# Attention, a gated MLP and an eight-expert layer on one core: a unit's keys and queries issued earlier, a spread of embeddings issued elsewhere

## The chip, the cores and the metric

The kernel runs on one core of a Trainium2 chip: TensorE (PE) for matrix products, VectorE (DVE), ScalarE (ACT), GpSimd (POOL), and SyncE (SP), which here issues nearly all transfers. The metric is the device time of one execution in microseconds; the comparison is between medians of runs.

## The reference

Three layers follow each other, all in float32.

```
scores = (q @ k^T) / sqrt(64) + bias(head, distance)   # only 0 <= distance < 128
x   = softmax(scores) @ v                              # 4 x 8 heads x 576 x 64 -> 2304 x 512
h   = x @ w_in                                         # 512 -> 2048
y   = (h * clip(h + 3, 0, 6) / 6) @ w_out              # 2048 -> 512
logits = (y/|y|) @ (emb/|emb|)^T / tau                 # 8 experts
e   = argmax(logits);  gate = softmax(logits)[e]
out = gate * (relu(y @ w1[e]) @ w2[e])                 # 512 -> 1024 -> 512, each token by its expert
```

## The kernel before

The 2304 tokens are cut into nine chunks of 256. Attention is done in units: a unit is one chunk and one pair of heads, so a chunk has four units, and unit n belongs to chunk n // 4. Units 0 to 7 (chunks 0 and 1, class `Early`) come from staged blocks. Units from 8 on (class `Unit`) load their own keys `kr`, queries `qr` and values `vr` in small pieces (`load_k`, `load_q`, `load_v`; L562 for keys and queries, L582 and L584 for values). Each of these tiles has two buffers, so a unit's load waits until the unit two before it has given its tile back.

A unit's path is: DVE transposes the keys to `kT` (L590) and the queries to `qT` (L594), ACT scales `qT` (L601), PE makes the scores `sc_ps` (L610), DVE and ACT make the softmax (L620 to L643), PE transposes it ("flips", L649), ACT and POOL bring it into order, and PE multiplies it with the values (`acc`, L675). PE does the flips of one unit, the values of the unit before it and the scores of the unit after it as one group.

The first MLP product is gemm1 (`h_ps`, L720; plain in chunk 0, L707), the second gemm2 (`y_ps`, L773; plain L764). A block of gemm1 goes through a relu on ACT (L730), a gate on DVE (L740) and a split into a high and a low part, `gh` on ACT (L744) and `gl` on DVE (L750), before gemm2 can take it. Weights are split the same way (L349 on ACT, L355 on DVE).

Behind a chunk's last gemm2 ACT copies its rows to `ys` (L792), SP stores them (L797), and the chunk is routed. For chunks 0 to 6 the logits are dot products on DVE (L834) of the rows with the normalised embeddings, which a spread (`spread`, L828) brings to all 128 partitions: a transfer of 1 MB for each half of the experts, so two per chunk. A spread's target `en_all` comes from the pool `w` of 17 large buffers, in which weight pieces live too. Then come `choose`, `ranks` (L880) and `place`.

The order of the work is made in two ways. For the opening (chunks 0 and 1, units 8 to 12, and unit 13 as far as its scores) the function `plan` holds a list of tasks with engine, duration, rank, needs and buffers taken and given; a small simulation runs them, the ready task of lowest rank first, and the order that it finds is what ACT, DVE and SP are given. Loads of units in it run up to `AHEAD_UNITS`, in the order of the ranks `UNIT_LOADS`; the two spreads of chunk 0 are the tasks `("issue spread", x)`. All later steps are put into `todo` at a place by number (`at(step, ...)`) and follow behind the whole list; PE keeps the written order throughout, and each engine works its own list strictly in order. There the spreads of chunk c stand at `g + loads[x]`, where `g = ends(c)` is the chunk's end, `DOTS` gives `loads = (-3.5, 4.5)`, and the chunk's rows are stored at `g`.

Of the kernel before, what the change touches and what calls it, by code (L numbers as in the profile page):

```python
# [16 lines left out]
SP = mybir.EngineType.SP  # L17
# [22 lines left out]
SPLIT_RANK = (322.3, 398.0, 346.4, 387.6, 346.1, 414.2, 437.7, 461.4, 636.9, 424.0, 421.1, 490.0, 548.3, 371.5, 669.2, 694.1)  # L40
CONST_RANK = (40.0, 50.0)

AHEAD_UNITS = 14

EARLY_CHUNKS = 2
WEIGH = (1, 1, 1, 0, 1, 1, 0, 1)
# [6 lines left out]
UNIT_8 = (95.0, 150.0, 96.0)  # L53
EMBED = (96.0, 97.0)
SOFT_1, DOTS_0 = 250.0, 2000.0
UNIT_LOADS = (80.0, 81.0, 82.0, 83.0, 84.0, 85.0)
FIRST = (16.97, 1.91, 3.35)


# [38 lines left out]
def tile_kernel(  # L98
# [17 lines left out]
    NE = w1.shape[0]  # L116
# [78 lines left out]
    for kinds in ((2, 2), (2, 0), (2, 1), (1, 2), (0, 2)):  # L195
        tables[kinds] = t = const.tile([128, 192], BF16, name="table%d%d" % kinds)
        for h, kind in enumerate(kinds):
            r = slice(64 * h, 64 * h + 64)
# [959 lines left out]
    def at(step, fn, *args):  # L1158
        todo[step].append((fn, args))
# [8 lines left out]
    def ends(c, i=NF2 - 1):  # L1168
        return 0.0 if c == 0 else begins(2) if c == 1 else begins(c, i) + FIRST[2]
# [8 lines left out]
    route_0 = Route(0)  # L1178

    def plan():  # L1180
# [19 lines left out]
        for n in range(len(pieces)):  # L1200
            r = PIECE_RANK[n]
# [5 lines left out]
        for n, u in enumerate(units[:n_early]):  # L1207
            c, p = u.c, u.p
            r = UNIT_RANK[n]
# [18 lines left out]
        for i in range(NF2):  # L1228
            r, d = GEMM_RANK[0][i], GEMM_RANK[1][i]
# [5 lines left out]
        for n in range(len(pieces)):  # L1235
            kind, i = pieces[n]
            r = SPLIT_RANK[n]
# [5 lines left out]
        task(("constants",), "SP", 1.6, CONST_RANK[0], [("issue", "st", 8)], ["w"], ["w"], constants)  # L1243
        for n in range(n_early, AHEAD_UNITS):
            u = units[n]
# [4 lines left out]
        def step(name, engine, cost, rank, needs, takes, gives, fn, *args, lag=0.12):  # L1250
            task(name, engine, cost, rank, needs, takes, gives, fn, args, lag)
# [4 lines left out]
        for n in range(n_early, last_unit + 2):  # L1256
            u, key = units[n], ("unit", n)
            first = n == n_early
            r = UNIT_8[0] if first else SOFT_1 + n
# [5 lines left out]
            r = UNIT_8[2] if first else SOFT_1 - 10  # L1265
# [26 lines left out]
        for x in ORDER_1:  # L1292
            before = line[-1:]
            if x == "u":
# [3 lines left out]
                r = SOFT_1 - 20 + i  # L1298
# [33 lines left out]
            step(("row store", t), "SP", 0.55, 0.0, [("row", t)], [], [], route_0.store, t)  # L1332
        step(("norms",), "ACT", 1.5, 1900.0, [("row", 1)], ["f"], [], route_0.norms)
        for x in range(2):
            step(("issue spread", x), "SP", 0.55, 90.0, [("en", "store"), ("issue", "st", 15)] + ([("dots", NE // 2 - 1)] if x else []), ["w"], [], route_0.spread, x)
            step(("spread", x), "DMA", 4.8, 0.0, [("issue spread", x)], [], [], None, lag=1.0)
        for e in range(NE):
            x, y = divmod(e, NE // 2)
# [43 lines left out]
    for n, u in enumerate(units[n_early:], n_early):  # L1382

        t0, t1, t2 = (group(n + x) for x in range(3))
        turn, norm, early, vearly = PARTS
        if n >= AHEAD_UNITS:
            at(t0 - early, u.load)
# [23 lines left out]
    for c in range(NCH - 1):  # L1411
        g = ends(c)
        if c < NCH - 2:
            loads, *halves, d2, d3 = DOTS
            if c == 0:
                g, r = FIRST[0], route_0
            else:
                r = Route(c)
                at(g, r.rows)
                at(g + 0.3, r.norms)  # L1420
                for x in range(2):
                    at(g + loads[x], r.spread, x)
                for e in range(NE):
                    x, y = divmod(e, NE // 2)
                    at(g + halves[x][0] + halves[x][1] * y, r.dots, e)
            at(g + d2 * (c > 0), r.choose)
            at(g + d3 * (c > 0) + PLACE_C * (c == 0), r.ranks)
            at(g + d3 * (c > 0) + PLACE_C * (c == 0), r.place)
            continue
        r = Route(c)  # L1430
        at(g, r.rows)
        d = ROUTE
        assert 0 < d[0] <= d[1] <= d[2] < d[2] + TOTAL < d[3]
        at(g + d[0], r.flip, 0)
        at(g + d[1], r.flip, 1)
        at(g + d[1], r.norms)
        at(g + d[2], r.logits)
        at(g + d[2] + TOTAL, r.total)
        at(g + d[2] + TOTAL, r.choose)
        at(g + d[3], r.ranks)  # L1440
        at(g + d[3], r.place)
    g = begins(NCH - 1)
# [19 lines left out]
    g = ends(NCH - 1)  # L1462
# [8 lines left out]
    r = Route(NCH - 1)  # L1471
# [34 lines left out]
    for j in range(1, NE):  # L1506
# [6 lines left out]
        if j == 1:  # L1513
            s = PLACE_1
            loads = [s[0] + s[1] * i for i in range(4)]
            splits = [s[2] + s[3] * i for i in range(8)]
            ids, gets, turns = LATE[0] + 0.05, [s[4] + s[5] * t for t in range(n)], [s[8] + s[9] * t for t in range(n)]
        else:
            s = [x + b - 16 for x in NEXT]
            s[5], s[7], s[9] = NEXT[5], NEXT[7], NEXT[9]  # L1520
            loads = [s[0], s[1], s[2], s[3]]
# [155 lines left out]
```

## Time and profile before

| | |
|---|---|
| Median of 3 runs | 780.51 us (778.58 to 782.57) |
| The profiled execution | 778.85 us |
| its span | 777.1 us |
| PE busy | 748.5 us (96%) |
| DVE busy | 522.6 us (67%) |
| ACT busy | 383.8 us (49%) |
| POOL busy | 195.7 us (25%) |
| mean granted clock of TensorE | 0.989 |

The span goes from the first to the last instruction of the profiled execution, whose own time is 1.75 us longer. PE is the engine with the most work; its matmuls are pipelined, so a busy PE is not PE at its peak. What matters for a change of order is where an engine stands idle and what ended the idle time. Granted clock 1.00 is 2.4 GHz, 0.50 is 1.2 GHz.

### The profile page before, as it was taken

The page shows a single profiled execution, that of the slowest core. Times are in us where ns is not written, and L with a number is a line of the kernel's source. Part 1 is how long each engine was busy: PE and PEld are TensorE (multiplying, and loading weights), DVE is VectorE, ACT ScalarE, POOL GpSimd, SP SyncE. Part 2 cuts the span into 40 slices and gives each one's busy share as a digit, 9 for nine tenths or more (in the row PEclk, how much of TensorE's full clock was granted, in tenths as well). Part 3 has the DMA queues.
Part 4 walks back from the last instruction along what each step waited for, and adds up shares of the span by engine and source line. Part 5 has one row for each costly group of instructions (what it writes and reads, how often), then busy time and mean ns, then how long its engine had stood idle before and what let it go on. Part 6 is the DMA issues. An engine that isn't in the chain of part 4 may idle for free.

```text
span 777.1 us, 15993 instructions
## 1 busy us (share of the span) xinstructions
PE 748.5 (96%) x5740; PEld 659.8 (85%) x5740; DVE 522.6 (67%) x1528; ACT 383.8 (49%) x896; POOL 195.7 (25%) x349
## 2 busy tenths in 40 slices
PE   8999999959999999999999999999989999999995
PEld 6566678848888888888888889888889999999994
DVE  4999999885778668688687783356636636645620
ACT  6958665543454544645544542447435544543510
POOL 3000023431241242241422422030323122223211
PEclk9999999979999999999999999999999999999999
DMA  9987242353544443345353220078177446546200
GB/s 211 346 287 210 56 111 43 100 117 87 113 92 132 108 126 72 92 122 136 66 140 98 85 65 2 29 215 276 36 265 255 150 155 198 197 160 215 89 27 28
DMA packets 159110, 103.20 MB, mean 133 GB/s; under 512 B 119419, under 2 KB 135931, under 8 KB 157232
## 3 DMA queue, kind: packets, MB, share of 16 engines
q1 hardware_dynamic: 155280, 92.53, 42.2%
q0 software_dynamic: 3744, 9.58, 3.7%
q8 instruction: 47, 0.77, 0.4%
q14 instruction: 39, 0.32, 0.1%
HBM read 87.71 MB, written 14.47 MB: 131 GB/s over the span
## 4 chain that ended last, share of the span: by engine, by line
PE 67%; DMA 11%; DVE 8%; issue 7%; SPq 3%; ACT 2%; POOL 1%; POOLq 0%; DVEq 0%; ACTq 0%
PE y_ps L773 21%; PE h_ps L720 21%; PE ps_u L1043 7%; PE ps_o L1067 4%; PE ps_z L1125 3%; PE acc L675 3%; DMA out_dram<-ob,ids 2%; PE sc_ps L610 2%; DMA ids<-slots 2%; DMA xg<-ybuf,ids 2%; DMA wst<-in_moe_w_out_dram 2%; DMA slots<-pays,dest 2%; PE ps_pt L649 1%; SPq L562 1%; DVE w L335 1%
## 5 line engine op out<-in xcount | busy, mean ns | idle before, releaser
L720 PEld LDWEIGHTS h_ps<-xs,w_i 128*128 128x128 f32 x1536 | 192.4, 191 | 6.1 <-issue 1.2
L720 PE MATMUL h_ps<-xs,w_i 128*128 128x256 f32 x1536 | 195.2, 283 | 0.0
L773 PE MATMUL y_ps<-w_o,gh 128*128 128x512 f32 x512 | 164.1, 402 | 0.3 <-ACT gh L744 0.3
L664 POOL TENSOR_SCALAR_AFFINE_SELECT ph<-ph 64x128 f32<-64x128 f32 x224 | 95.5, 426 | 193.9 <-ACT ph L656 156.6
L773 PEld LDWEIGHTS y_ps<-w_o,gh 128*128 128x128 f32 x512 | 92.4, 190 | 24.4 <-issue 6.0
L1043 PE MATMUL ps_u<-x,w_e 128*128 128x280 f32 (+5 forms) x768 | 105.4, 294 | 0.0
L162 DVE TENSOR_TENSOR w_e<-st,w_e 128x1024 fp32r<-128x1024 f32 x64 | 76.5, 1217 | 38.6 <-ACT w_e L161 38.6
L773 PE MATMUL y_ps<-w_o,gl 128*128 128x512 f32 x256 | 100.6, 393 | 1.2 <-DVE gl L750 1.2
L1043 PEld LDWEIGHTS ps_u<-x,w_e 128*128 128x128 f32 x768 | 100.5, 189 | 0.2
L834 DVE CUSTOM_DVE_ANT_0 junk<-ys,en_all 128x512 f32<-128x512 f32 x112 | 77.2, 690 | 19.2 <-DMA en_all<-en_rows 10.5
L730 ACT ACTIVATE u<-h_ps,three 128x512 f32<-128x512 f32 x72 | 49.1, 682 | 75.1 <-PE h_ps L720 50.9
L1067 PE MATMUL ps_o<-hs,w_e 128*128 128x280 f32 (+4 forms) x576 | 78.5, 295 | 0.0
L1067 PEld LDWEIGHTS ps_o<-hs,w_e 128*128 128x128 f32 x576 | 76.6, 188 | 0.0
L161 ACT CAST w_e<-st 128x1024 fp32r<-128x1024 f32 x64 | 65.4, 1048 | 17.8 <-DMA st<-in_moe_w_dram 6.3
L740 DVE SCALAR_TENSOR_TENSOR u<-u,h_ps 128x512 f32<-128x512 f32 x72 | 49.2, 684 | 36.3 <-ACT u L730 35.6
L744 ACT CAST gh<-u 128x512 fp32r<-128x512 f32 x64 | 39.7, 620 | 54.1 <-DVE u L740 53.7
L750 DVE TENSOR_TENSOR gl<-u,gh 128x512 fp32r<-128x512 f32 x64 | 45.0, 703 | 26.0 <-ACT gh L744 26.0
L633 ACT ACTIVATE pt<-pt,nm 128x128 f32<-128x128 f32 x112 | 44.1, 395 | 34.3 <-DVE pt L626 33.7
L773 PEld LDWEIGHTS y_ps<-w_o,gl 128*128 128x128 f32 x256 | 48.4, 189 | 13.3 <-DVE gl L750 2.5
L1142 POOL DMA_INDIRECT out_dram<-ob,ids x23 | 30.3, 1317 | 113.5 <-DVE ob L1141 101.9
L1051 ACT ACTIVATE hs<-ps_u 128x280 fp32r<-128x280 f32 (+5 forms) x64 | 25.6, 403 | 45.0 <-PE ps_u L1043 44.0
L1052 DVE SCALAR_TENSOR_TENSOR hs<-ps_u,hs 128x280 fp32r<-128x280 f32 (+5 forms) x64 | 27.8, 443 | 20.6 <-ACT hs L1051 20.2
(185 smaller groups left out, 994.7 us busy)
## 6 DMA issues: line engine op xcount, KB each, us to landing
st<-in_moe_w_dram SPq DMA_DIRECT2D x32, 512.0 KB
st<-in_moe_w_dram SPq DMA_DIRECT2D x16, 1024.0 KB
en_all<-en_rows SPq DMA_DIRECT2D x14, 1024.0 KB
wst<-in_moe_w_in_dram SPq DMA_DIRECT2D x8, 1024.0 KB
wst<-in_moe_w_out_dram SPq DMA_DIRECT2D x8, 1024.0 KB
ybuf<-ys SPq DMA_DIRECT2D x18, 256.0 KB
out_dram<-empty SPq DMA_DIRECT2D x18, 256.0 KB
kr<-in_k_dram SPq DMA_DIRECT2D x48, 48.0 KB
```

Of the source, the lines that this page charges most:

```text
L161: nc.scalar.copy(hi, src)
L162: eng.tensor_tensor(out=lo, in0=src, in1=words(hi), op=ALU.subtract)
L633: nc.scalar.activation(out=x, in_=x, func=AF.Exp, scale=-1.0, bias=nm[:, j:j + 1], accum_out=sums[h][:, j:j + 1])
L664: nc.gpsimd.affine_select(out=out, in_=x, compare_op=ALU.is_gt if out is prev else ALU.is_ge, fill=0.0, base=0, pattern=[[0, 2], [-1 if ou ...
L720: nc.tensor.matmul(hp[:, f, :], lhsT=w[:, a, kk, f * 128:(f + 1) * 128], rhs=xs[:, b, kk, :], start=(n == 0), stop=(n == 3 * KD - 1),)
L730: nc.scalar.activation(out=u, in_=hp, func=AF.Relu, bias=three, scale=1.0)
L740: V.scalar_tensor_tensor(out=u, in0=u, scalar=6.0, in1=h_t[c, i], op0=ALU.min, op1=ALU.mult)
L750: V.tensor_tensor(out=gl, in0=g, in1=words(gh), op=ALU.subtract)
L773: nc.tensor.matmul(y_t[c][t], lhsT=g[a][:, f, t * 128:(t + 1) * 128], rhs=w[:, b, f, :], start=(i == 0 and f == 0 and n == 0), stop=(i == ...
L834: V.tensor_tensor_reduce(out=self.junk, in0=self.ys[t], in1=self.en[:, e % (NE // 2), :], scale=1.0, scalar=0.0, op0=ALU.mult, op1=ALU.add ...
L1043: nc.tensor.matmul(ps, lhsT=w[:, a, kk, (f % 2) * 128:(f % 2) * 128 + 128], rhs=x[:, b, kk, c0:c1], start=(n == 0), stop=(n == 3 * KD - 1),)
L1067: nc.tensor.matmul(ps, lhsT=ws_t[j, 4 + f // 2][:, a, f % 2, d * 128:(d + 1) * 128], rhs=hs[:, b, f, 0:width(j)], start=(n == 0), stop=(n ...
```

## The change

Three numbers and one expression change. `AHEAD_UNITS` goes from 14 to 15, with one more rank in `UNIT_LOADS`: the keys and queries of unit 14 become tasks of the opening's list, where before they were a step of `todo`. Its transpositions stay in `todo`. The two spreads of chunk 0 get rank 70 instead of 90, which puts the first of them before the loads of unit 9 (rank 81). And the first spread of chunk 1 stands at `g + 0.6` instead of `g - 3.5`, that is behind the storing of that chunk's rows at `g` and not before it; the spreads of later chunks stay.

```diff
--- before.py
+++ after.py
@@ -40,7 +40,7 @@
 SPLIT_RANK = (322.3, 398.0, 346.4, 387.6, 346.1, 414.2, 437.7, 461.4, 636.9, 424.0, 421.1, 490.0, 548.3, 371.5, 669.2, 694.1)
 CONST_RANK = (40.0, 50.0)
 
-AHEAD_UNITS = 14
+AHEAD_UNITS = 15
 
 EARLY_CHUNKS = 2
 WEIGH = (1, 1, 1, 0, 1, 1, 0, 1)
@@ -53,7 +53,7 @@
 UNIT_8 = (95.0, 150.0, 96.0)
 EMBED = (96.0, 97.0)
 SOFT_1, DOTS_0 = 250.0, 2000.0
-UNIT_LOADS = (80.0, 81.0, 82.0, 83.0, 84.0, 85.0)
+UNIT_LOADS = (80.0, 81.0, 82.0, 83.0, 84.0, 85.0, 86.0)
 FIRST = (16.97, 1.91, 3.35)
 
 
@@ -1332,7 +1332,7 @@
             step(("row store", t), "SP", 0.55, 0.0, [("row", t)], [], [], route_0.store, t)
         step(("norms",), "ACT", 1.5, 1900.0, [("row", 1)], ["f"], [], route_0.norms)
         for x in range(2):
-            step(("issue spread", x), "SP", 0.55, 90.0, [("en", "store"), ("issue", "st", 15)] + ([("dots", NE // 2 - 1)] if x else []), ["w"], [], route_0.spread, x)
+            step(("issue spread", x), "SP", 0.55, 70.0, [("en", "store"), ("issue", "st", 15)] + ([("dots", NE // 2 - 1)] if x else []), ["w"], [], route_0.spread, x)
             step(("spread", x), "DMA", 4.8, 0.0, [("issue spread", x)], [], [], None, lag=1.0)
         for e in range(NE):
             x, y = divmod(e, NE // 2)
@@ -1419,7 +1419,7 @@
                 at(g, r.rows)
                 at(g + 0.3, r.norms)
                 for x in range(2):
-                    at(g + loads[x], r.spread, x)
+                    at(g + (loads[x] if c > 1 or x else 0.6), r.spread, x)
                 for e in range(NE):
                     x, y = divmod(e, NE // 2)
                     at(g + halves[x][0] + halves[x][1] * y, r.dots, e)
```

SP's queue where the opening's last weight piece (`wst_813`) is loaded, before; `kr_820` and `qr_860` are the keys and queries of unit 9, `kr_1004` and `qr_1052` those of unit 11, `en_all` is a spread, `ybuf` a store of chunk 0's rows:

```order
L315 DMA wst_813<-in_moe_w_out_dram 128x2x1024
L562 DMA kr_820<-in_k_dram 32x6x32 x8
...
L562 DMA kr_1004<-in_k_dram 32x6x32 x8
L562 DMA qr_1052<-in_q_dram 32x2x32 x4
L562 DMA qr_1052<-in_q_dram 32x6x32 x4
L828 DMA en_all_1107<-en_rows_129 128x2048
L797 DMA ybuf_128<-ys_1104 128x512
```

and now, with unit 9 in `kr_826` and `qr_865`, unit 11 in `kr_1033` and `qr_1059`:

```order
L315 DMA wst_813<-in_moe_w_out_dram 128x2x1024
L828 DMA en_all_820<-en_rows_129 128x2048
L562 DMA kr_826<-in_k_dram 32x6x32 x8
...
L562 DMA kr_1033<-in_k_dram 32x6x32 x8
L562 DMA qr_1059<-in_q_dram 32x2x32 x4
L562 DMA qr_1059<-in_q_dram 32x6x32 x4
L797 DMA ybuf_128<-ys_1125 128x512
```

The first spread of chunk 0 has moved from behind unit 11's loads to the place ahead of unit 9's.

SP's queue at the seam between the list and what follows it, before; `en_all_1614` is the second spread of chunk 0, `en_all_1829` the first of chunk 1, `kr_1831` and `qr_1836` are unit 14, `kr_1927` and `qr_1932` unit 15, and the `ybuf` stores are chunk 1's rows:

```order
L584 DMA vr_1565<-in_v_dram 128x64 x2
L828 DMA en_all_1614<-en_rows_129 128x2048
L584 DMA vr_1664<-in_v_dram 128x3x64 x2
L828 DMA en_all_1829<-en_rows_129 128x2048
L562 DMA kr_1831<-in_k_dram 32x12x32 x4
L562 DMA qr_1836<-in_q_dram 32x8x32 x4
L584 DMA vr_1855<-in_v_dram 128x3x64 x2
L797 DMA ybuf_128<-ys_1915 128x512
L797 DMA ybuf_128<-ys_1918 128x512
L562 DMA kr_1927<-in_k_dram 32x12x32 x4
L562 DMA qr_1932<-in_q_dram 32x8x32 x4
L584 DMA vr_2072<-in_v_dram 128x3x64 x2
```

and now, with unit 14 in `kr_1614` and `qr_1731`, unit 15 in `kr_1925` and `qr_1930`, the second spread of chunk 0 in `en_all_1665` and the first of chunk 1 in `en_all_1935`:

```order
L584 DMA vr_1566<-in_v_dram 128x64 x2
L562 DMA kr_1614<-in_k_dram 32x12x32 x4
L828 DMA en_all_1665<-en_rows_129 128x2048
L584 DMA vr_1683<-in_v_dram 128x3x64 x2
L562 DMA qr_1731<-in_q_dram 32x8x32 x4
L584 DMA vr_1853<-in_v_dram 128x3x64 x2
L797 DMA ybuf_128<-ys_1913 128x512
L797 DMA ybuf_128<-ys_1916 128x512
L562 DMA kr_1925<-in_k_dram 32x12x32 x4
L562 DMA qr_1930<-in_q_dram 32x8x32 x4
L828 DMA en_all_1935<-en_rows_129 128x2048
L584 DMA vr_2072<-in_v_dram 128x3x64 x2
```

Unit 14's keys have gone ahead of chunk 0's second spread, its queries ahead of unit 13's values, and chunk 1's first spread behind unit 15's loads.

DVE's list at the transpositions of unit 14 (`kT_1940`, `qT_1942`), before; L689 and L162 end unit 12, L750 is a split of chunk 2's second block, L834 are dot products of chunk 1:

```order
L689 TENSOR_TENSOR both_2027<-acc_2011,part_2025 128x256
L750 TENSOR_TENSOR gl_1977<-u_1972,gh_1975 128x512
L590 STREAM_TRANSPOSE kT_1940<-kr_1831 128x384
L893 CAST dest_1984<-den_1982 128x2
L162 TENSOR_TENSOR xs_2029<-both_2027,xs_2029 128x256
L834 ISA junk_1922,lg_1937<-ys_1915,en_all_1829 128x512
L834 ISA lg_1937 128x1
L834 ISA junk_1922,lg_1937<-ys_1918,en_all_1829 128x512
L834 ISA lg_1937 128x1
L834 ISA junk_1922,lg_1937<-ys_1915,en_all_1829 128x512
L834 ISA lg_1937 128x1
L834 ISA junk_1922,lg_1937<-ys_1918,en_all_1829 128x512
```

and now; L869 to L871 choose the experts of chunk 0, `pt_1839` and `pt_1846` are the two halves of unit 13's softmax, L740 is the gate of chunk 2's first block:

```order
L869 TENSOR_TENSOR pick_1899<-pick_1899,order_136 128x16
L590 STREAM_TRANSPOSE kT_1940<-kr_1614 128x384
L639 TENSOR_SCALAR rs_1856<-sums0_152 128x2
L870 TENSOR_REDUCE mx_1898<-pick_1899 128x2
L875 TENSOR_TENSOR sh_1900<-sh_1900,rn_1139 128x16
L640 RECIPROCAL rs_1856<-rs_1856 128x2
L871 TENSOR_TENSOR oh_1901<-pick_1899,mx_1898 128x16
L594 STREAM_TRANSPOSE qT_1942<-qr_1731 128x256
...
L740 SCALAR_TENSOR_TENSOR u_1891<-u_1891,h_ps_1866 128x512
L643 TENSOR_SCALAR pt_1846<-pt_1846,rs_1861 128x128 x2
```

Both transpositions have moved from among chunk 1's dot products into the normalisation of unit 13, and the gate stands ahead of that unit's last normalisation.

## Rows read from the trace of the kernel before

**Rows 1.** Waits of PE over the span: us in total, times, longest

```profile
PE sc_ps L610 <- ACT qT L601: 7.9, 1, 7.9
PE ps_x L1013 <- DMA xg<-ybuf,ids: 4.7, 3, 2.0
```

**Rows 2.** Busy time by stretch, 175 to 300 us: sums, clock, DMA

```profile
175.00:300.00 125.00, 125.00 (x1078) 111.10 (x1078) 88.21 (x331) 58.16 (x163) 35.41 (x80) 1.00 0.45 109
```

**Rows 3.** Timeline of PE: start, us, instruction, idle before and its releaser

```profile
89.47 1.09 PE L524 MATMUL acc<-ph,stage 128*64 128x128 f32 x12
...
104.58 0.50 PE L773 MATMUL y_ps<-w_o,gl 128*128 128x512 f32 x1 [0.75 <-DVE gl L750]
...
159.50 0.64 PE L649 MATMUL ps_pt<-ident,pt 128*128 128x128 f32 x4
...
168.86 1.56 PE L610 MATMUL sc_ps<-kT,qT 64*64 64x192 f32 x16 [7.91 <-ACT qT L601]
```

**Rows 4.** Timeline of DVE, around units 13 and 14, and one spread later

```profile
146.01 0.68 DVE L834 CUSTOM_DVE_ANT_0 junk<-ys,en_all 128x512 f32<-128x512 f32 x1
...
147.35 0.68 DVE L740 SCALAR_TENSOR_TENSOR u<-u,h_ps 128x512 f32<-128x512 f32 x1
...
153.61 0.43 DVE L162 TENSOR_TENSOR xs<-both,xs 128x256 fp32r<-128x256 f32 x1 [0.47 <-ACT xs L161]
...
157.55 0.48 DVE L643 TENSOR_SCALAR pt<-pt,rs 128x128 f32<-128x128 f32 x2
...
164.06 0.56 DVE L590 STREAM_TRANSPOSE kT<-kr 128x384 f32<-128x384 f32 x1
...
167.83 0.44 DVE L594 STREAM_TRANSPOSE qT<-qr 128x256 f32<-128x256 f32 x1
...
173.72 0.49 DVE L643 TENSOR_SCALAR pt<-pt,rs 128x128 f32<-128x128 f32 x2
...
294.04 0.79 DVE L834 CUSTOM_DVE_ANT_0 junk<-ys,en_all 128x512 f32<-128x512 f32 x1 [2.95 <-DMA en_all<-en_rows]
```

**Rows 5.** Timeline of SP's issues: opening, unit 14, and one spread later

```profile
73.16 1.27 SPq L315 DMA_DIRECT2D wst<-in_moe_w_out_dram  x1
...
79.67 3.64 SPq L562 DMA_DIRECT2D qr<-in_q_dram  x8
...
135.72 0.38 SPq L828 DMA_DIRECT2D en_all<-en_rows  x1
139.84 0.92 SPq L584 DMA_DIRECT2D vr<-in_v_dram  x2
152.83 0.34 SPq L828 DMA_DIRECT2D en_all<-en_rows  x1
...
160.77 2.28 SPq L562 DMA_DIRECT2D kr<-in_k_dram  x4
163.41 1.79 SPq L562 DMA_DIRECT2D qr<-in_q_dram  x4
...
288.74 0.34 SPq L828 DMA_DIRECT2D en_all<-en_rows  x1
```

**Rows 6.** Busy time of short stretches before and behind the long wait

```profile
150.07:153.68 3.61, 3.61 (x40) 2.83 (x33) 3.03 (x10) 0.98 (x4) 3.27 (x6) 1.00 0.00 0
150.83:153.68 2.85, 2.85 (x16) 2.36 (x13) 2.31 (x8) 0.51 (x2) 2.58 (x5) 1.00 0.00 0
168.86:174.60 5.74, 5.74 (x28) 4.22 (x29) 3.63 (x19) 1.65 (x8) 0.00 (x0) 0.60 0.18 26
174.60:177.47 2.87, 2.87 (x25) 2.87 (x24) 0.42 (x2) 0.00 (x0) 0.00 (x0) 1.00 0.11 17
```

**Rows 7.** Timeline of ACT: a weight piece, a relu, rows of chunk 1

```profile
74.72 1.16 ACT L323 ACTIVATE w<-wst 128x1024 f32<-128x1024 f32 x1
...
146.34 0.69 ACT L730 ACTIVATE u<-h_ps,three 128x512 f32<-128x512 f32 x1 [0.39 <-PE h_ps L720]
...
153.49 1.08 ACT L792 ACTIVATE ys<-y_ps 128x512 f32<-128x512 f32 x2
```

## The prediction

> **What bounds the kernel now.** I read the page first: the span is 777.1 us and this execution took 778.85, so 1.75 us lie around the span. Then the waits of PE over the whole span: one is far longer than all others, 7.9 us in a single piece before the scores of a unit, put down to ACT's scaled queries qT [rows 1]. Then the busy time by stretch: from 175 to 300 us PE is busy in all of 125.00 us [rows 2], so what PE loses before 175 is not made up behind it, and a loss that goes should arrive at the end.
>
> The place is in the timeline of PE: flips at 159.50, values behind them, and the scores only at 168.86, with 7.91 us idle ahead [rows 3]. Counted by blocks of scores, these are unit 14's. DVE turned its keys at 164.06 and its queries at 167.83, with dot products of chunk 1 between them [rows 4]. Before that comes SP: between the values' load at 139.84 and the spread of embeddings at 152.83, the first half of chunk 1's, it issued nothing; that spread needs the buffer which chunk 0's last dot product gives back, and unit 14's keys and queries stand behind it in SP's queue [rows 5]. So the chain is: a buffer held by chunk 0's dots, the spread at the head of SP's queue, the keys, DVE, ACT, PE. And the stall costs more than its length: in the scores and the gemm2 after it, 168.86 to 174.60, the granted clock was 0.60, a mean over its levels of 1.2 and 2.4 GHz, and they took 5.74 us; the same pieces took 3.61 one group earlier, at 1.00 [rows 6].
>
> **The change part by part.**
> *Unit 14's keys and queries in the opening's list.* The same eight issues and the same bytes go to another place. The keys now stand ahead of chunk 0's second spread, which left at 135.72; the queries follow unit 12's values, which left at 139.84 [rows 5], so at about 141. The scores' turn comes where the idle time began, at 168.86 - 7.91 = 160.95. On DVE both transpositions move into the softmax of unit 13. The stall goes, and with it the slow clock: 7.91 + (5.74 - 3.61) = 10.04 us.
>
> *What is late next.* It is DVE, at unit 13's flips. Before, the last of its normalisations (L643) ended at 157.55 + 0.48 = 158.03, 1.47 before the flips [rows 3, 4]. Now three things more stand ahead of it. Two dot products of chunk 0 (146.01 to 147.35, so 1.34) come behind the gate instead of before it; the gate can start when the relu is done, 146.34 + 0.69 = 147.03, instead of at 147.35: 1.34 - 0.32 = 1.02 later [rows 4, 7]. The keys' transposition adds 0.56, the queries' 0.44, and the gate of chunk 2's first block, now ahead of the last L643, 0.68 like the one at 147.35. The 0.47 in which DVE waited for ACT's split before 153.61 [rows 4] is filled by dots. So 158.03 + 1.02 + 0.56 + 0.44 + 0.68 - 0.47 = 160.26, and PE waits some 0.7 at the flips. Bounds: 0, if part of this chain moves up with PE, and 1.2, if the 0.47 is not filled. I take 0.6, a little under the sum, since the durations listed overlap.
>
> *Chunk 1's first spread behind that chunk's rows.* No instruction is added. SP stores the rows of chunk 1, loads unit 15 and only then issues the spread: rows ready at 153.49 + 1.08 = 154.57 [rows 7], stores about 0.9, unit 15's keys and queries 2.28 + 1.79 plus gaps [rows 5], so near 160. From a spread's issue to the dot product that it released there is one clean pair: 288.74 to 294.04, 5.30 us [rows 4, 5]. It lands near 165.3. In DVE's list these dots now follow unit 14's softmax: its scores end near 160.95 + 0.6 + 0.8 = 162.4, from the end of the scores to the last normalisation it took 168.86 + 1.56 = 170.42 to 173.72 + 0.49 = 174.21 [rows 3, 4], so 3.8, and two splits and some transpositions lie between: DVE comes to the dots at about 168, 2.7 after the landing. Behind three of them stands a split of g that a gemm2 needs: done near 171.6; wanted after two gemm2 (2.85 each) and two gemm1 (2.87 each) [rows 6], and one set of flips, values and scores (160.95 - 159.50 + 0.76, so 2.2), at 162.4 + 11.4 + 2.2 = 176.0. It is covered; without that cover each microsecond would cost one. The eight dots themselves (5.4 at two in 1.34) ran beside the stall until now; they go into DVE's free time, of which 125.00 - 88.21 = 36.79 us lie between 175 and 300 [rows 2]. I cost them at nothing.
>
> *Chunk 0's first spread at rank 70.* It goes from behind unit 11's queries to the place right behind the last weight load, which left at 73.16 [rows 5]. It holds one of the 17 large buffers for some 30 us more, so the last two weight pieces are converted a little later, and splits of weights move ahead of unit 8's softmax on DVE. PE's list is rearranged too: the last plain gemm2 now stands behind chunk 1's second gemm1. In this stretch PE waited 0.75 for DVE's split of g at 104.58 [rows 3]. That split now has one gemm2 more of time, so the wait should go; on the other hand chunk 1's second gemm1 wants its low weights within some tenths of when DVE has them. Bounds: 0.75 gained, 0.7 lost. I take 0.5 gained, the side of the wait that the trace shows.
>
> *The sum.* 10.04 - 0.6 + 0.5 = 9.9 us: 778.85 - 9.9 = 768.9 us for an execution like the profiled one. That one lies 1.66 under the median of the three runs shown, 780.51; for a median of runs I expect 780.51 - 9.9 = 770.6 us.
>
> **The rivals.**
> *The wait moves.* The stall leaves unit 14, and smaller ones come up at unit 13's flips or at a gemm2 of chunk 2: DVE works in order, and a spread that lands late holds up the normalisations and gates behind its dots. For it: DVE waited 2.95 for a spread before 294.04 [rows 4], and 0.6 is counted already. Against it: chunk 0's second spread would leave near 137.7 and land near 143, some 4.7 before DVE wants it. Two spreads as late as that one, chunk 0's second and chunk 1's first, cost 2 x 2.95 = 5.9, less the 0.6: 770.6 + 5.3 = 775.9 us.
> Two rules of the Trainium skill speak for this rival, in "DMA: Bandwidth & Descriptors": descriptors of one ring are consumed in the ring's order (section "Queues, rings and completion order"), and pieces under 512 bytes stay below line rate (section "Specifications"). By them the spread starts only behind unit 15's pieces of 128 bytes; an estimate from that page's 435 GB/s, halved, gives 1.5 us for their 320 KB and a landing near 166.8 instead of 165.3, still before 168. No row of before shows this order, and the sum is the same by either.
>
> *Nothing comes of it.* The gain is given back, since another chain than PE's list sets a later point. For it: PE waits three times for gathered rows, 4.7 us [rows 1]. Against it: those rows follow from what PE itself finished, and from 175 to 300 there is no gap into which a gain could go [rows 2]. Time: 780.5 us.
>
> *Slower.* The first spread, now ahead of unit 9's loads, finds no free large buffer and holds SP until unit 7's values free four of them, 89.47 + 1.09 = 90.6 [rows 3], 16.2 after the 73.16 + 1.27 = 74.4 at which its turn comes [rows 5]. Unit 9's queries, whose issue ended at 79.67 + 3.64 = 83.3 [rows 5], would leave at 99.5 and be there near 102; by the new list DVE wants them near 92.5, its weight splits standing behind. It would lose 10 us, unit 10's loads some 3 more, and the slow clock 2.1: 15 against 9.9, so 780.51 + 5.1 = 785.6 us. It decides from some 10 us of such waiting on. Against it: at 74.72 ACT began to convert the next weight piece into a fresh large buffer right behind its work before [rows 7], so one was free.
>
> **How the numbers follow.** Forecast 0.76 (own range 767 to 773), moved wait 0.13 (775.9), nothing 0.07 (780.5), slower 0.04 (785.6). Half a per cent, 3.9 us, is about what a measurement of this kernel can tell from no change. Faster, below 776.6, is the forecast and nearly all of the moved wait: 0.88; the same 0.08; slower 0.04. The range starts at the best sum, 10.04 + 0.75 = 10.8 under the lowest run shown, 778.58, which is 767.8, rounded down to 767, and ends at 776, just behind the moved wait, which leaves out 0.11 above and some 0.06 below.
>
> **What would show it.** In the profile after: no idle time of microseconds before the scores at L610; granted clock 1.00 from 160 to 175; unit 14's keys on SP near 136 and chunk 1's first spread near 160; DVE at the keys' transposition near 157; a wait of PE at the flips (L649) near 159, under 1.2; none at L773 near 104; PE without gaps from 175 on, all some 10 us earlier. Against it would stand: DVE idle before L834 with a spread as its end, SP idle before the spread near 74, or a PE wait of over 2 us anywhere between 75 and 200.

## The result and the profile after

The changed kernel took 771.75 us (median of 7 runs, 771.13 to 776.75), the kernel before 779.97 us (7 runs, 778.58 to 782.57): a ratio of 0.9901, 95% interval 0.9876 to 0.9926, so 8.2 us faster. Forecast were 770.6 us and a gain of 9.9 us. The time came within 1.2 us of the forecast, the gain fell 1.7 short of it; one term of the sum was wrong by 5.6 us, and two others were off the other way. The profiled execution took 771.75 us with a span of 769.9, against 778.85 and 777.1 before, so 7.2 us are to be found in the traces.

The timeline of PE after the change, as in [rows 3]: start, duration, engine, line, operation, and in brackets the idle time and what ended it.

```profile
104.57 0.60 PE L649 MATMUL ps_pt<-ident,pt 128*128 128x128 f32 x4
...
157.11 0.64 PE L649 MATMUL ps_pt<-ident,pt 128*128 128x128 f32 x4
157.68 0.89 PE L675 MATMUL acc<-ph,vr 64*64 64x192 f32 x24
158.39 0.83 PE L610 MATMUL sc_ps<-kT,qT 64*64 64x192 f32 x16
...
162.00 3.04 PE L720 MATMUL h_ps<-xs,w_i 128*128 128x256 f32 x24
...
170.49 0.60 PE L649 MATMUL ps_pt<-ident,pt 128*128 128x128 f32 x4
172.40 0.54 PE L675 MATMUL acc<-ph,vr 64*64 64x192 f32 x2 [1.30 <-POOL ph L664]
174.74 1.00 PE L675 MATMUL acc<-ph,vr 64*64 64x192 f32 x19 [1.80 <-POOL ph L664]
...
177.00 1.22 PE L773 MATMUL y_ps<-w_o,gh 128*128 128x512 f32 x2
```

Two things are to be seen. The stall ahead of unit 14's scores is gone: they stand at 158.39 without idle time, where before they stood at 168.86 behind 7.91 us [rows 3]. And one group later there is a new wait, 3.10 us in two pieces, at the values of unit 13; GpSimd's selects `ph` ended it. The clock falls behind this one as it did behind the old one. The busy time by stretch shows it in the gemm2 that follows (columns: length, then busy time and count of PE, PEld, DVE, ACT, POOL, the granted clock, DMA share, GB/s):

```profile
157.11:162.00 4.89, 4.89 (x59) 3.92 (x59) 3.84 (x16) 2.95 (x7) 2.80 (x3) 1.00 0.78 239
...
177.00:181.00 4.00, 4.00 (x13) 3.20 (x13) 3.87 (x21) 2.43 (x10) 0.83 (x3) 0.70 0.57 127
```

From unit 13's flips to the next gemm1 it was 159.50 to 174.60 before [rows 3, 6], 15.10 us, and is 4.89 now at clock 1.00: 10.21 gained. The later gemm2, of the same size as the one that took 2.85 [rows 6], took 4.00 at 0.70.

GpSimd's timeline after tells what the selects waited for:

```profile
159.12 1.21 POOL L896 DMA_INDIRECT slots<-pays,dest  x1 [1.78 <-DVE dest L893]
160.64 1.40 POOL L896 DMA_INDIRECT slots<-pays,dest  x1 [0.30 <-issue]
162.05 0.53 POOL L664 TENSOR_SCALAR_AFFINE_SELECT ph<-ph 64x128 f32<-64x128 f32 x1
171.56 6.40 POOL L664 TENSOR_SCALAR_AFFINE_SELECT ph<-ph 64x128 f32<-64x128 f32 x15 [8.98 <-DMA slots<-pays,dest]
```

The placements of chunk 0 (L896, two transfers through a list of addresses) come first, one select of unit 13 follows, and the second select waits 8.98 us until the placements have landed. Before the change the eight selects came first:

```profile
161.61 4.24 POOL L664 TENSOR_SCALAR_AFFINE_SELECT ph<-ph 64x128 f32<-64x128 f32 x8 [2.78 <-ACT ph L656]
166.16 1.37 POOL L896 DMA_INDIRECT slots<-pays,dest  x1 [0.30 <-POOL ph L664]
```

So the program lists:

```
GpSimd before: L664 x8 (unit 13) | L896 x2 | L664 x16 (units 14, 15)
GpSimd after:  L896 x2 | L664 x24 (units 13, 14, 15)
```

A select reads nothing of `slots`, and why it waits for that transfer no run here shows; in all the kernels below whose placements of chunk 0 were still under way it is the second select behind them that waits.

The order of SP's and DVE's rows is as forecast, and they stand 2.2 to 2.7 us earlier than the forecast's times, as PE's flips of unit 13 do (157.11 against 159.50). SP issued unit 14's keys before chunk 0's second spread, and chunk 1's first spread behind unit 15's queries:

```profile
133.37 1.91 SPq L562 DMA_DIRECT2D kr<-in_k_dram  x4
135.88 0.34 SPq L828 DMA_DIRECT2D en_all<-en_rows  x1
...
155.91 1.79 SPq L562 DMA_DIRECT2D qr<-in_q_dram  x4
157.81 0.39 SPq L828 DMA_DIRECT2D en_all<-en_rows  x1
```

DVE turned both, finished unit 13's softmax just in time, and came to chunk 1's dot products without waiting for the spread:

```profile
154.29 0.58 DVE L590 STREAM_TRANSPOSE kT<-kr 128x384 f32<-128x384 f32 x1
...
155.20 0.45 DVE L594 STREAM_TRANSPOSE qT<-qr 128x256 f32<-128x256 f32 x1
...
156.81 0.48 DVE L643 TENSOR_SCALAR pt<-pt,rs 128x128 f32<-128x128 f32 x2
...
165.78 0.68 DVE L834 CUSTOM_DVE_ANT_0 junk<-ys,en_all 128x512 f32<-128x512 f32 x1
```

### The profile page after: what moved, and what is told of

Same layout as the page of the kernel before. It is cut to its first block, busy times and chain, and to the rows that moved or that the text cites. A ratio compares the mean times of both kernels' runs of the same rounds, so it can differ in the third digit from the quotient of the medians.

```text
span 769.9 us, 15998 instructions
## 1 busy us (share of the span) xinstructions
PE 748.2 (97%) x5740; PEld 659.8 (86%) x5740; DVE 523.0 (68%) x1528; ACT 384.1 (50%) x896; POOL 188.8 (25%) x349
## 4 chain that ended last, share of the span: by engine, by line
PE 73%; DMA 11%; issue 6%; DVE 6%; SPq 2%; POOL 2%; ACT 1%; POOLq 0%; DVEq 0%; ACTq 0%
PE h_ps L720 21%; PE y_ps L773 21%; PE ps_u L1043 8%; PE ps_o L1067 6%; PE ps_z L1125 3%; PE acc L675 3%; PE h_ps L707 3%; DMA st<-in_moe_w_dram 3%; DMA out_dram<-ob,ids 2%; PE sc_ps L610 2%; PE y_ps L764 2%; DMA xg<-ybuf,ids 1%; DMA wst<-in_moe_w_out_dram 1%; PE ps_pt L649 1%; DMA slots<-pays,dest 1%
## 5 line engine op out<-in xcount | busy, mean ns | idle before, releaser
L773 PE MATMUL y_ps<-w_o,gh 128*128 128x512 f32 x512 | 164.4, 403 | 0.8 <-ACT gh L744 0.8
L664 POOL TENSOR_SCALAR_AFFINE_SELECT ph<-ph 64x128 f32<-64x128 f32 x224 | 90.6, 405 | 186.7 <-ACT ph L656 140.9
L773 PEld LDWEIGHTS y_ps<-w_o,gh 128*128 128x128 f32 x512 | 92.2, 190 | 25.5 <-issue 5.4
L162 DVE TENSOR_TENSOR w_e<-st,w_e 128x1024 fp32r<-128x1024 f32 x64 | 76.5, 1217 | 39.2 <-ACT w_e L161 39.1
L773 PE MATMUL y_ps<-w_o,gl 128*128 128x512 f32 x256 | 100.6, 393 | 0.9 <-DVE gl L750 0.8
L834 DVE CUSTOM_DVE_ANT_0 junk<-ys,en_all 128x512 f32<-128x512 f32 x112 | 77.1, 688 | 19.7 <-DMA en_all<-en_rows 11.1
L740 DVE SCALAR_TENSOR_TENSOR u<-u,h_ps 128x512 f32<-128x512 f32 x72 | 49.2, 683 | 31.7 <-ACT u L730 30.9
L750 DVE TENSOR_TENSOR gl<-u,gh 128x512 fp32r<-128x512 f32 x64 | 45.7, 715 | 25.0 <-ACT gh L744 25.0
L773 PEld LDWEIGHTS y_ps<-w_o,gl 128*128 128x128 f32 x256 | 48.4, 189 | 12.9 <-DVE gl L750 2.2
```

Source lines behind the costliest of these rows:

```text
L162: eng.tensor_tensor(out=lo, in0=src, in1=words(hi), op=ALU.subtract)
L664: nc.gpsimd.affine_select(out=out, in_=x, compare_op=ALU.is_gt if out is prev else ALU.is_ge, fill=0.0, base=0, pattern=[[0, 2], [-1 if ou ...
L740: V.scalar_tensor_tensor(out=u, in0=u, scalar=6.0, in1=h_t[c, i], op0=ALU.min, op1=ALU.mult)
L750: V.tensor_tensor(out=gl, in0=g, in1=words(gh), op=ALU.subtract)
L773: nc.tensor.matmul(y_t[c][t], lhsT=g[a][:, f, t * 128:(t + 1) * 128], rhs=w[:, b, f, :], start=(i == 0 and f == 0 and n == 0), stop=(i == ...
L834: V.tensor_tensor_reduce(out=self.junk, in0=self.ys[t], in1=self.en[:, e % (NE // 2), :], scale=1.0, scalar=0.0, op0=ALU.mult, op1=ALU.add ...
```

## The experiments

All times are medians, each beside runs of the kernel before on the same chip (its median there was 779.97 us in the first result and 776.36 to 777.46 in the runs below). The ratio to it is what can be compared across chips.

| kernel | loads | shift | rank 70 | ratio to before | 95% interval |
|---|---|---|---|---|---|
| changed | yes | yes | yes | 0.9901, again 0.9917 | 0.9876 to 0.9926, 0.9899 to 0.9934 |
| changed, selects first | yes | yes | yes | 0.9852, again 0.9857 | 0.9828 to 0.9876, 0.9838 to 0.9876 |
| no shift | yes | no | yes | 0.9868 | 0.9842 to 0.9893 |
| no rank 70 | yes | yes | no | 0.9907 | 0.9887 to 0.9927 |
| loads alone | yes | no | no | 0.9920 | 0.9897 to 0.9942 |
| no loads | no | yes | yes | 0.9970 | 0.9949 to 0.9992 |
| rank 70 alone | no | no | yes | 0.9976 | 0.9964 to 0.9989 |
| shift alone | no | yes | no | 0.9998 | 0.9984 to 1.0012 |

"Loads" are unit 14's keys and queries in the opening's list, "shift" is chunk 1's first spread behind that chunk's rows.

**The selects first.** Only GpSimd's list differs from the changed kernel's.

```diff
+            for y in x * (not placed):
+                tc.add_manual_dep(y.ins, selected[-1].ins.name, PLACED, reason="the selects first")
...
-            at(g + d3 * (c > 0) + PLACE_C * (c == 0), r.place)
+            at(g + d3 * (c > 0) + 2.6 * (c == 0), r.place)
```

(`selected` holds the last select that was written; `x` are the two placements. The lines that fill `selected` are left out here.)

> The changed kernel with one thing undone, GpSimd's order: the two placements of chunk 0 (L896) stand behind unit 13's eight selects again, as they did before the change; the lists of the other four engines are those of the changed kernel. Theory A (the placement's landing, which the second select of unit 13 waits for, costs PE 3.1 us of waiting at unit 13's values and some 2.5 us of slow clock): that wait goes, the selects end near 162, gemm2 behind unit 14's flips keeps clock 1.00, and the time is 771.75 - 5.6 = 766.1 us. Theory B (the landing is waited for anyway; the wait then stands at unit 14's second select, and PE waits for it there, at unit 14's values): 771 to 772 us. Theory C (PE's time there is taken back later by another wait, for chunk 1's spread or for gathered rows): 769 to 771 us, with a new wait of over 2 us behind 175.

Measured: 765.06 us against 776.36, so 11.3 faster. GpSimd and PE in its trace:

```profile
160.77 3.29 POOL L664 TENSOR_SCALAR_AFFINE_SELECT ph<-ph 64x128 f32<-64x128 f32 x8 [2.11 <-ACT ph L656]
164.36 1.21 POOL L896 DMA_INDIRECT slots<-pays,dest  x1 [0.30 <-POOL ph L664]
165.88 1.01 POOL L896 DMA_INDIRECT slots<-pays,dest  x1 [0.30 <-issue]
173.05 0.64 POOL L664 TENSOR_SCALAR_AFFINE_SELECT ph<-ph 64x128 f32<-64x128 f32 x1 [6.16 <-ACT ph L656]
174.14 3.49 POOL L664 TENSOR_SCALAR_AFFINE_SELECT ph<-ph 64x128 f32<-64x128 f32 x7 [0.45 <-DMA slots<-pays,dest]
```

```profile
171.82 0.60 PE L649 MATMUL ps_pt<-ident,pt 128*128 128x128 f32 x4
172.35 0.89 PE L675 MATMUL acc<-ph,vr 64*64 64x192 f32 x24
...
176.71 3.04 PE L720 MATMUL h_ps<-xs,w_i 128*128 128x256 f32 x24
```

The wait did go to unit 14's second select, as theory B has it, but it is 0.45 us there and PE does not feel it. From unit 14's flips to the next gemm1 PE needs 176.71 - 171.82 = 4.89 us; in the changed kernel it was 181.00 - 170.49 = 10.51. The difference, 5.62, is what the new wait cost in that execution: 3.10 of idle time and 2.52 in which PE counts as busy for longer. Of these 2.52, 1.11 are the gemm2 at clock 0.70 (4.00 against 2.89); the other 1.41 lie in the values and scores before it, where the clock was 0.78 from 174.74 to 177.00 and the selects also came one by one, and the trace does not part the two. Theory A holds, except that not all of the 2.5 us is shown to be slow clock, and from 95 to 330 us this kernel has no wait of PE at all.

**No shift.**

```diff
-                    at(g + (loads[x] if c > 1 or x else 0.6), r.spread, x)
+                    at(g + loads[x], r.spread, x)
```

> The changed kernel with one part undone: chunk 1's first spread is issued ahead of that chunk's rows again; unit 14's keys and queries stay in the opening's list and chunk 0's first spread at rank 70. GpSimd's order then has unit 13's selects ahead of the placement. Theory A (the two parts in the opening bring all of the gain, the shift only brings the wait of GpSimd): as with the selects put first, 771.75 - 5.6 = 766.1 us, no stall ahead of unit 14's scores. Theory B (the spread holds SP's queue until chunk 0's last dot product near 150, and unit 15's keys or DVE's dot products come late for it): a new wait of 2 to 8 us at unit 15's scores or at a gemm2 of chunk 2, 768 to 775 us.

Measured: 766.08 us against 776.36; the intervals of this kernel and the last overlap. Its trace has no wait of PE from 95 to 330 us either. The spread did hold SP (it left at 151.99) and DVE waited for it, but only 0.87 us:

```profile
158.20 0.69 DVE L834 CUSTOM_DVE_ANT_0 junk<-ys,en_all 128x512 f32<-128x512 f32 x1 [0.87 <-DMA en_all<-en_rows]
```

Theory A holds. The trace also suggests why the shift turns GpSimd's list round. Here chunk 1's first dots stand between the arithmetic of chunk 0's placement on DVE, and the addresses `dest` (L893) are made at 163.19, behind ACT's copy of the flips at 160.19, which the selects want. With the shift those dots are later, and in the changed kernel `dest` comes before the copy:

```profile
158.65 0.17 DVE L893 CAST dest<-den 128x2 int32<-128x2 f32 x1
...
159.00 0.64 ACT L656 COPY ph<-ps_pt 128x256 f32<-128x256 f32 x2
```

The placement is ready first, and stands first. The lists are fixed before the program runs, so these times on the chip make this likely and do not show it.

**The shift alone.** The kernel before with the line of the change that moves the spread.

> The kernel before with one part alone: chunk 1's first spread behind that chunk's rows; nothing changed in the opening. Theory A (the spread at the head of SP's queue is the whole cause of the stall, where unit 14's loads are written does not matter): SP issues unit 14's keys near 141, the stall and its slow clock go (10.0 us), the opening keeps its 0.75 us wait: 780 - 10.0 = 770 us. Theory B (unit 14's loads must leave ahead of unit 13's softmax, so they have to be in the opening's list): a wait of 3 to 8 us stays ahead of unit 14's scores, 774 to 780 us.

Measured: 776.48 us against 776.36, no change. SP issued unit 14's keys at 140.95, long before they were wanted, so the block on SP is gone; yet PE waited, and twice:

```profile
164.41 0.88 PE L610 MATMUL sc_ps<-kT,qT 64*64 64x192 f32 x16 [3.35 <-ACT qT L601]
...
202.21 0.17 PE L880 MATMUL rk<-oh,earlier 128*128 128x16 bf16 x1 [2.78 <-DVE oh L871]
```

```profile
162.30 0.83 DVE L750 TENSOR_TENSOR gl<-u,gh 128x512 fp32r<-128x512 f32 x1 [0.61 <-ACT gh L744]
...
163.39 0.43 DVE L594 STREAM_TRANSPOSE qT<-qr 128x256 f32<-128x256 f32 x1
...
175.86 0.65 DVE L834 CUSTOM_DVE_ANT_0 junk<-ys,en_all 128x512 f32<-128x512 f32 x1
```

The queries lie ready, but their transposition stands in DVE's list behind a split that waits for ACT, so 3.35 us of the stall stay, and the scores and gemm2 behind them took 5.25 us at clock 0.67 (3.61 at 1.00 in [rows 6]). The kernel before fits this: DVE was not idle ahead of either transposition of unit 14 [rows 4], so it was their place in its list that held them, and not the landing of the keys. Without SP's block the queries' transposition moved from 167.83 to 163.39; with the loads in the opening's list it comes at 155.20 in the changed kernel. The spread leaves at 161.24, chunk 1's first dot product comes at 175.86, and its ranks come late for PE. Between the first and second of these points it is 4.9 us ahead of the kernel before (unit 14's flips at 178.16 against 183.09), and behind the second 0.2 (unit 16's at 209.79 against 210.02). Neither theory had the second wait; B is the nearer one, since the loads' place in the opening's list decides where the transpositions stand.

**The loads alone.** The kernel before with `AHEAD_UNITS = 15` and the seventh rank.

> The kernel before with one part alone: unit 14's keys and queries in the opening's list; the spreads of chunks 0 and 1 where they were. Theory A (taking unit 14's loads out from behind the spread is enough): the stall and its slow clock go (10.0 us), the opening keeps its 0.75 us wait, GpSimd's order is that of before: 780 - 10.0 = 770 us. Theory B (the stall moves one unit on, to unit 15's keys behind the same spread): a wait of 3 to 8 us ahead of unit 15's scores, 774 to 780 us.

Measured: 770.76 us against 776.36, 5.6 faster, not 10. The stall is gone and did not move to unit 15; but here the wait at unit 13's flips is there:

```profile
160.07 0.18 PE L880 MATMUL rk<-oh,earlier 128*128 128x16 bf16 x1 [1.24 <-DVE oh L871]
161.00 0.17 PE L881 MATMUL rk<-seen,ones 128*128 128x16 bf16 x1 [0.75 <-DVE seen L872]
...
161.93 0.52 PE L649 MATMUL ps_pt<-ident,pt 128*128 128x128 f32 x2 [0.48 <-DVE pt L643]
162.38 1.33 PE L675 MATMUL acc<-ph,vr 64*64 64x192 f32 x24
163.47 1.52 PE L610 MATMUL sc_ps<-kT,qT 64*64 64x192 f32 x16
```

1.24 + 0.75 + 0.48 = 2.47 us, and the values and scores behind them are slow (1.33 and 1.52 instead of 0.89 and 0.83; the granted clock was 0.73 from 161.93 to 168.31). Its DVE made chunk 0's last eight dot products in one block from 151.26 to 157.2, right ahead of unit 13's softmax; with rank 70 they were under way at 145.27. The second spread left at 143.12 here and at 135.88 in the changed kernel. DVE's trace shows no wait for it, so the dots were late by their place in the list; that the later spread put them there is likely and not tested.

**No rank 70.**

```diff
-            step(("issue spread", x), "SP", 0.55, 70.0, ...
+            step(("issue spread", x), "SP", 0.55, 90.0, ...
```

> The changed kernel with one part undone: chunk 0's first spread at rank 90 again (unit 14's loads in the opening and chunk 1's shifted spread stay). GpSimd's order is then four selects of unit 13, the two placements, the other twenty selects. Theory A (rank 70 is what keeps DVE ahead: without it chunk 0's last four dot products stand in one block ahead of unit 13's softmax, PE waits some 2.4 us at that unit's ranks and flips as with the loads alone, and the placement's landing is waited for as well): loads alone gained 5.6 us over the kernel before, the landing takes 4 to 6 back, so 0 to 2 us faster than the kernel before. Theory B (rank 70 matters only through its 0.75 us in the opening): 1 us behind the changed kernel, so some 7 us faster than the kernel before.

Measured: 769.92 us against 777.46, 7.5 faster, as much as the changed kernel. Theory B had the size, but not the reason; theory A had half of the reason. The same waits as with the loads alone are there (1.24, 0.7 and 0.5 us), and the second wait of theory A is not: the second half of unit 13's selects waited for the placements, but only to 173.22.

```profile
162.52 1.36 POOL L664 TENSOR_SCALAR_AFFINE_SELECT ph<-ph 64x128 f32<-64x128 f32 x4 [4.20 <-ACT ph L656]
...
166.71 0.28 POOL L664 TENSOR_SCALAR_AFFINE_SELECT ph<-ph 64x128 f32<-64x128 f32 x1
173.22 1.78 POOL L664 TENSOR_SCALAR_AFFINE_SELECT ph<-ph 64x128 f32<-64x128 f32 x3 [6.23 <-DMA slots<-pays,dest]
```

They were done at 175.0, and PE wanted them at 175.30. The profiled execution is the fastest of the four (767.98 to 771.43 us), and PE's clock did not fall behind the three waits as it did with the loads alone:

```profile
161.46 0.53 PE L649 MATMUL ps_pt<-ident,pt 128*128 128x128 f32 x2 [0.49 <-DVE pt L643]
161.91 0.89 PE L675 MATMUL acc<-ph,vr 64*64 64x192 f32 x24
162.62 0.83 PE L610 MATMUL sc_ps<-kT,qT 64*64 64x192 f32 x16
```

From the last of the waits to the next gemm1 it took 4.82 us at 1.00 here, and 6.38 at 0.73 there.

Rank 70 is worth some 4 us where GpSimd's wait does not reach PE (0.9907 here against 0.9852 with the selects first, 0.9920 with the loads alone against 0.9868 without the shift). GpSimd's wait is worth 4.7 to 5.6 us, by the experiments with the selects first. In the comparison of this kernel with the changed one the two hide each other.

**No loads, and rank 70 alone.** Each is one part undone, or one done, by the lines above.

> The changed kernel with one part undone: unit 14's keys and queries out of the opening's list, behind unit 12's values on SP; chunk 0's first spread stays at rank 70, chunk 1's shifted. Theory A (as with the shift alone, DVE's list puts the queries' transposition behind a split that waits for ACT, and chunk 1's dots come late for its ranks; rank 70 adds its 1 to 2 us in the opening): PE waits about 3 us ahead of unit 14's scores and 3 us ahead of chunk 1's ranks, 1 to 2 us faster than the kernel before. Theory B (with the dot products of chunk 0 earlier, DVE comes to the transposition in time): no wait there, 7 to 10 us faster.

> The kernel before with one part alone: chunk 0's first spread at rank 70. Theory A (it frees the opening of its 0.75 us and one smaller wait, and does nothing for the stall): the stall of 8 us ahead of unit 14's scores stays, 1 to 2 us faster than the kernel before. Theory B (the opening's gain is swallowed by the stall, since SP's block ends with chunk 0's last dot product, which does not move): the same time as before, within 0.5 us, and a stall of 9 us.

Measured: 775.11 and 775.31 us against 777.46. Without the loads PE waits 3.2 us ahead of unit 14's scores and 2.7 ahead of chunk 1's ranks, as with the shift alone; with rank 70 alone the stall stays at 8.49 us. Theory A holds in both, with a gain a little above its 1 to 2 us: rank 70 gives some 2 us, and nothing that it does removes the stall.

**A lighter spread.** This kernel leaves out three of the four embeddings of chunk 1's first spread, so part of the routing: it sends many more rows to one expert, its whole time (2101.78 us) says nothing, and only 150 to 185 us are read.

```diff
+            m = 1 if (self.c, half) == (1, 0) else NE // 2; src = en_rows[NE // 2 * half:NE // 2 * half + m, :].rearrange("(o e) d -> o (e d)", o=1)
+            nc.sync.dma_start(out=self.en[:, 0:m].rearrange("p e d -> p (e d)"), in_=src.to_broadcast([128, m * DM]))
...
+                    out=self.junk, in0=self.ys[t], in1=self.en[:, 0 if self.c == 1 and e < NE // 2 else e % (NE // 2), :],
```

> The changed kernel, but chunk 1's first spread brings one embedding row (256 KB over the partitions) instead of four (1 MB), and chunk 1's dot products with the first four experts all use that one row; so part of the routing of chunk 1 is left out, and only the stretch from 150 to 185 us is to be read. Lists of SP, GpSimd and PE are the same there. Theory A (the placement's few packets queue behind the spread's 1 MB, which moved at 300 to 440 GB/s as it was issued): the placement lands in 6 to 8 us instead of 10.8, unit 13's selects begin 3 to 4 us earlier, PE's wait at its values shrinks from 3.1 us to under 1 us. Theory B (the landing is long by itself, as the first of its kind in the kernel, or behind other loads): 10 to 11 us, the wait stays at 3 us.

Measured, GpSimd and PE:

```profile
158.99 1.21 POOL L896 DMA_INDIRECT slots<-pays,dest  x1 [1.79 <-DVE dest L893]
160.51 1.40 POOL L896 DMA_INDIRECT slots<-pays,dest  x1 [0.30 <-issue]
...
168.41 7.81 POOL L664 TENSOR_SCALAR_AFFINE_SELECT ph<-ph 64x128 f32<-64x128 f32 x15 [5.95 <-DMA slots<-pays,dest]
```

```profile
171.97 0.54 PE L675 MATMUL acc<-ph,vr 64*64 64x192 f32 x4 [0.56 <-POOL ph L664]
172.71 0.65 PE L675 MATMUL acc<-ph,vr 64*64 64x192 f32 x15 [0.19 <-POOL ph L664]
```

The placements, issued at the same time to 0.13 us, landed in 7.8 us instead of 10.8. GpSimd waited 5.95 us instead of 8.98, and PE 0.75 instead of 3.10. From unit 14's flips to the next gemm1 PE needed 6.66 us, at clock 1.00, where the changed kernel needed 10.51. It is one execution beside one, and the second profile of the changed kernel (the last experiment) has 9.6 us where the first has 10.8; so the bytes of the spread account for 1.8 to 3.0 us of the landing, and theory A holds for these. That 7.8 us stay with a quarter of the spread's bytes is not explained by it; no run here takes the units' small loads out of that stretch.

The Trainium skill, "DMA: Bandwidth & Descriptors", section "Anatomy of one DMA — SWDGE (gpsimd) path", gives a transfer issued by GpSimd about 2.0 us plus its bytes at some 436 GB/s, which for a placement's few bytes would be 2 us. The trace differs: no landing of chunk 0's placements was under 6.3 us, and the measurement decides. By an estimate from that page the second placement would have landed near 162.04 + 2 = 164, and the seven selects of unit 13 that are left would have ended near 167.5 (seven took 3.49 with the selects first). PE, which wants them at 170.49 + 0.53 = 171.0, would not have waited.

**The two side by side.** The changed kernel and the one with the selects first, on one chip.

> The changed kernel as it is, on one chip with the version below. Theory A: 0.990 of the kernel before, as in the first result (0.988 to 0.993), with the 9 us wait of GpSimd's second select and 3 us of PE's wait at unit 13's values. Rival (the wait of GpSimd was a matter of that one profiled execution, since the landing is short in others): no such wait here, and the time equal to that of the version below.

> The changed kernel with unit 13's selects ahead of chunk 0's placements on GpSimd, beside the changed kernel on the same chip. Theory A: 5 to 6 us less than the changed kernel, 0.983 to 0.988 of the kernel before. Rival (the gain seen first came from the opening or from the chip): within 2 us of the changed kernel.

Measured: 770.08 and 765.36 us, against 777.05. The wait is in this execution too (the select waited 7.76 us, PE 2.2), and the version without it is 4.7 us faster than the changed kernel and 11.7 faster than the one before. From unit 14's flips to the next gemm1 PE needed 9.74 us, 4.85 more than the 4.89 without the wait, so trace and medians agree on the price.

## Why the prediction was right, and where not

In profiled spans the forecast was 10.04 - 0.6 + 0.5 = 9.9. Measured was 10.2 + 0 + 2.4 - 5.6 = 7.0, of the 7.2 by which the spans differ.

- *The stall and its slow clock, 10.04.* Measured 10.21. The size held; the chain (SP's block, the keys, DVE, ACT) only in part. The shift alone takes SP's block away, and 3.35 us of the stall with its slow clock stay. Before the change DVE was not idle ahead of either transposition; with the shift alone one of them stands behind a split that waits for ACT. So their place in DVE's list decided, and not the landing of the keys. What removed the stall is that the loads in the opening's list bring the transpositions forward. That all of it arrives behind 175 if nothing else comes held too, as the kernel with the selects first shows.
- *What is late next: DVE at unit 13's flips, 0.6.* Measured 0 in the changed kernel: the last L643 ended at 156.81 + 0.48 = 157.29, and the flips ran from 157.11 without a gap. That is the lower of the bounds that the step names. In the kernels with the loads and without rank 70 waits of 2.47 us do stand at this place, behind a block of chunk 0's dots; the step worked from the times at which the trace of before had these dots and did not ask what rank 70 does to them.
- *Chunk 1's spread, nothing.* Right for the dots and the transfer: issued at 157.81, first dot at 165.78 without waiting. Wrong as a whole, and this is the step that failed. It counted what the shift does to SP's and DVE's lists, and left out what stands behind DVE's: `dest` came 0.35 us ahead of the copy that the selects want, where before it came 3.39 behind (164.56 against 161.17); chunk 0's placements went ahead of the selects in GpSimd's list, and a select waited for a landing of 10.8 us. The price was 5.62 us in this execution and 4.85 in the second. The difference of the two programs shows the turned list; it was not read for GpSimd. The trace of before shows this kind of wait too, at placements of later chunks: five times a select waited for one, 24.7 us in all.

```profile
POOL ph L664 <- DMA slots<-pays,dest: 24.7, 5, 6.4
```

- *Rank 70, 0.5.* Unit 8's flips stood at 104.57 after the change, and before it here:

```profile
106.97 0.60 PE L649 MATMUL ps_pt<-ident,pt 128*128 128x128 f32 x4
```

  So the two profiled executions give 106.97 - 104.57 = 2.40. Unit 8's flips stand at a mean of 106.50 in the four profiles with rank 90 (105.73 to 107.08) and of 104.98 in the eight with rank 70 (104.42 to 105.93), so about 1.5 us are the change's and the rest is how this execution began. The 0.75 us wait at L773 is gone, as forecast; the term was too small.
- *The rivals.* "The wait moves" came true in part, by another engine: it was to come from two late spreads at 5.3 us net, and came from GpSimd at 5.6. What was named as evidence against the forecast, a PE wait of over 2 us between 75 and 200, is there: 3.10 us in two pieces in this execution, 2.18 in one piece in the second. "Slower" did not come: SP issued the spread at 73.71 without waiting for a buffer and went on to unit 9's keys at 74.56. "Nothing" did not come either. That the median still fell within 1.2 us of the forecast was luck: the opening gave more than was counted, the wait at the flips did not come, and the median of before was 779.97 and not the 780.51 from which the forecast started.

So the gain has a simple account: the loads remove the stall, rank 70 gives 1.5 to 2 us in the opening and keeps DVE ahead so that nothing follows at the flips, and the shift, once the other two are there, gains nothing that these runs can tell and turns GpSimd's list (all of it with both others there, half of it without rank 70, none of it without the loads). Undone (766.08), or with the list put right (765.06), the kernel is some 10 to 11 us faster than before; these two are not told apart.

## What to carry to other kernels

Compare the order of every engine, the idle ones first of all: an engine that is busy a quarter of the time can still hand the bottleneck its input late, when one of its instructions waits for a transfer's landing and others queue behind. A price read at one place, like the wait at the flips, belongs to the order in which it was read; parts of a change that move the same engine's work are to be costed together. And try the parts singly: two effects of 4 to 6 us were hidden in a comparison that said "the same".

## What the hardware showed

- The placements of chunk 0, a few bytes for each of 128 rows, landed 6.3 to 10.8 us after their issue in the eleven profiles of kernels that do all of the work. In the changed kernel's order the later landing took 10.8 and 9.6 us in two profiles beside a transfer of 1 MB, and 7.8 us in one beside a transfer of 256 KB.
- Two idle pieces of PE, 1.30 and 1.80 us, were followed by a granted clock of 0.78 over 2.26 us and of 0.70 over the next gemm2. In the kernel with the shift alone a single wait of 2.78 us was followed by 0.81 over 8.82 us; the same stretch took 7.01 us in the kernel with the selects first, so that wait cost 1.81 us beyond its own length.
- The same waits need not cost the same. Three of 1.24, 0.75 and 0.48 us were followed by 0.73 over 6.38 us in the profile of the loads alone; three of 1.24, 0.75 and 0.49 us, at the same place, by 1.00 over 4.82 us in the profile without rank 70. What made the difference no run here shows.
- Executions differ in how the opening goes: unit 8's flips stood at 104.57 and 105.93 in two executions of the changed kernel, and at 105.90 and 105.14 in two with the selects first, whose order on PE is the same. A term under 1.5 us in the opening is not to be read from a single pair of traces.
